# Channel attention on one core: the ones for the sums are loaded into TensorE once instead of before each matmul

## The chip, the cores and the metric

The kernel runs on 1 core of one Trainium2 chip. The metric is the device time in microseconds; a profiled execution also gives the span from the first to the last instruction, which is about 1.8 us shorter. A run counts as slow when it is over 1.5% above the fastest of the same kernel; the results quoted here come from the other, fast ones, except where the text says otherwise. A time or a ratio with two numbers in brackets behind it has its lowest and highest run, or its 95% interval, there. Runs that were submitted together ran on the same chip and share their runs of the kernel before.

## The reference, cut to what matters

```python
def reference(x, w1d):                 # x: 1 x 384 x 384 x 384, bf16;  w1d: 1 value
    g = jnp.einsum("bhwc->bc", x) / (H * W)      # mean of each channel
    s = _sigmoid(g * w1d[0])                     # (written as a convolution of length 1)
    return x * s[:, None, None, :]               # the gate
```

x has 113.25 MB. It has to be read once and written once, 226.5 MB in all, if the kernel does not need x a second time.

## The kernel before

It reads x once. It cuts the 1152 rows per partition into 27 blocks: 25 of 44 rows per partition, then 28 and 24. A block is 128 partitions by up to 16896 bf16 values (4224 KB) and sits in one of six slots of SBUF, the core's working memory. The gate is computed early, from block 0 alone, all blocks are multiplied with that, and the true gate is computed from all sums at the end. Should the two differ in bf16, a second pass over everything repairs the output. On this data they agree, and the second pass does not run.

TensorE makes the sums. A matmul of a 128x128 matrix of ones with 512 columns of a block adds up the partitions. The sums accumulate in PSUM, the memory in which the matmuls put their results: those of block 0 in three of its banks, those of all other blocks in three more. I call the 33 matmuls of a full block a burst.

```python
    def add_rows(place, n, group, first, last):
        n_wide = n * C // WIDE                       # WIDE = 512; 33 for a block of 44 rows
        start = place * C
        for i in range(n_wide):
            bank = acc[group][i % 3]
            plan.op("tensor",
                lambda e, i=i, bank=bank: e.matmul(
                    bank[:, :],
                    ones[:],                          # the weights: always the same ones
                    arena[:, start + i * WIDE : start + (i + 1) * WIDE],
                    start=first and i < 3,
                    stop=last and i >= n_wide - 3,
                ), ...)                               # (cut: what it reads and writes)
```

Each such call becomes two instructions on TensorE, a weight load and a matmul. The main loop, with the waits left to the planner:

```python
    add_rows(places[0], sizes[0], 0, True, True)      # block 0 -> early gate (cut)
    for k in range(1, len(sizes)):
        if k >= n_slots:
            j = k - n_slots
            put(places[j], ...)       # VectorE: gate block j in place; Scalar queue: store it
        if k >= BOTH:
            load(places[k], ...)      # Sync queue: load block k once the slot's store has landed
        add_rows(places[k], sizes[k], 1, k == 1, k == last)
```

So a slot goes through load, sum, gate and store, and the next load waits until the store has landed.

## Time and profile before

| | before |
|---|---|
| median of the first 3 runs | 531.62 us (531.5 to 532.85) |
| span of the profiled execution | 529.9 us |
| bytes moved, mean rate | 226.62 MB, 428 GB/s |
| TensorE matmuls, busy | 865, 246.9 us (47%) |
| TensorE weight loads, busy | 865, 96.4 us (18%) |
| VectorE busy | 241.2 us (46%) |

In the lines of the profile PE is TensorE's matmuls, PEld its weight loads, DVE VectorE, ACT ScalarE and POOL GpSimd; q1, q8 and so on are DMA queues, and SPq and ACTq the queues from which DMAs are issued. L186 is line 186 of the kernel.

From the page of the kernel before: the busy time of each engine; the share of time that the DMA engines were busy in 40 equal slices of the span, in tenths; what they moved; and the DMA queues with packets, bytes and share.

```profile
PE 246.9 (47%) x865; PEld 96.4 (18%) x865; DVE 241.2 (46%) x45; ACT 2.7 (1%) x4; POOL 0.3 (0%) x5
...
DMA  8999999999999999999999999999999999999997
...
DMA packets 8363, 226.62 MB, mean 428 GB/s; under 512 B 930, under 2 KB 930, under 8 KB 930
## 3 DMA queue, kind: packets, MB, share of 16 engines
q10 hardware_dynamic: 4466, 121.90, 53.4%
q1 hardware_dynamic: 3888, 104.60, 46.0%
q8 instruction: 6, 0.10, 0.1%
q14 instruction: 3, 0.02, 0.0%
```

The row of nines is the main reading: the DMA is the limit from the second slice to the last but one.

The costliest groups of the same page (line, engine, operation, shapes, count; then busy time, mean ns of one; then the idle time before them and what ended it):

```profile
L186 PE MATMUL acc<-arena,ones 128*128 128x512 bf16 x864 | 246.8, 457 | 242.3 <-DMA arena<-in_x_dram 242.3
L156 DVE TENSOR_TENSOR arena<-arena,s_early 128x16896 bf16<-128x16896 bf16 (+2 forms) x27 | 234.5, 8691 | 240.3 <-PE acc L186 236.1
L186 PEld LDWEIGHTS acc<-arena,ones 128*128 128x128 bf16 x864 | 96.3, 114 | 392.3 <-DMA arena<-in_x_dram 254.5
```

TensorE waits for loads to land about as long as it works, and VectorE waits for TensorE. Neither is the limit. The Sync queue's own waits show where a slot's time goes: it waits for stores to land before it may load again.

```profile
SPq L99 <- DMA out_dram<-arena: 454.2, 21, 63.1
```

Parts of the chain that ended last, in order of time (start, duration, what): the sums of block 0 near the start, and the sums of the last block with the comparison that follows them.

```profile
14.43 0.16 PE w_all L234
14.59 10.20 PE acc L186 x33
...
497.35 6.27 PE acc L186 x18
...
508.19 0.15 DVE redo L312
```

This chain ends with an instruction at 508 us although the span ends at 529.9: what runs after it are the last stores. In these windows over the end of the span the last two columns are the mean share of the 16 DMA engines that was busy, and GB/s.

```profile
520.00:526.00 6.00, 0.00 (x0) 0.00 (x0) 0.00 (x0) 0.00 (x0) 0.00 (x0) 0.50 0.96 414
526.00:528.00 2.00, 0.00 (x0) 0.00 (x0) 0.00 (x0) 0.00 (x0) 0.00 (x0) 0.50 0.39 166
528.00:536.00 8.00, 0.00 (x0) 0.00 (x0) 0.00 (x0) 0.00 (x0) 0.00 (x0) 0.76 0.01 5
```

### The profile page before, as it was taken

What the parts mean: (1) busy time and instruction counts of PE and PEld (TensorE: products, weight loads), DVE (VectorE), ACT (ScalarE), POOL (GpSimd) and SP (SyncE); (2) the same over time, 40 slices, a digit from 0 to 9 for tenths busy, and PEclk for the clock granted to TensorE, in tenths of its full rate; (3) what the DMA queues carried; (4) which work ended last, traced back from release to release, by engine and by line L of the source; (5) the groups of instructions that cost most, each with busy time, mean ns of one, the idle gap of its engine ahead of it and who ended that gap; (6) DMA issues with size and microseconds to landing.
All of it is one profiled execution on the core that took longest, in us unless ns stands there. A gap on an engine that the chain in (4) does not pass through costs nothing.

```text
span 529.9 us, 1954 instructions
## 1 busy us (share of the span) xinstructions
PE 246.9 (47%) x865; PEld 96.4 (18%) x865; DVE 241.2 (46%) x45; ACT 2.7 (1%) x4; POOL 0.3 (0%) x5
## 2 busy tenths in 40 slices
PE   0977174264274274364264274373263373374400
PEld 0333021121021121121021121121121121121100
DVE  0199824633624624623624615615614615617620
ACT  1000000000000000000000000000000000000000
POOL 0000000000000000000000000000000000000000
PEclk9988675786786875786786875776886876777665
DMA  8999999999999999999999999999999999999997
GB/s 357 430 427 412 446 429 431 446 412 444 434 426 446 413 443 444 416 444 431 429 445 416 441 439 421 446 414 441 444 416 446 427 431 444 424 429 431 444 416 331
DMA packets 8363, 226.62 MB, mean 428 GB/s; under 512 B 930, under 2 KB 930, under 8 KB 930
## 3 DMA queue, kind: packets, MB, share of 16 engines
q10 hardware_dynamic: 4466, 121.90, 53.4%
q1 hardware_dynamic: 3888, 104.60, 46.0%
q8 instruction: 6, 0.10, 0.1%
q14 instruction: 3, 0.02, 0.0%
HBM read 113.25 MB, written 113.25 MB: 427 GB/s over the span
## 4 chain that ended last, share of the span: by engine, by line
another core or an unknown queue 70%; DMA 16%; DVE 4%; PE 3%; issue 1%; SPq 1%; ACT 0%; ACTq 0%
DMA out_dram<-arena 8%; DMA arena<-in_x_dram 6%; PE acc L186 3%; DMA w_one<-in_w1d_dram 2%; DVE arena L156 2%; SPq L91 1%; DVE total L208 1%; ACT s_true L290 0%; ACT s_early L266 0%; DVE total L298 0%; DVE total L206 0%; DVE wrong L306 0%; ACTq L91 0%; SPq L99 0%
## 5 line engine op out<-in xcount | busy, mean ns | idle before, releaser
L186 PE MATMUL acc<-arena,ones 128*128 128x512 bf16 x864 | 246.8, 457 | 242.3 <-DMA arena<-in_x_dram 242.3
L156 DVE TENSOR_TENSOR arena<-arena,s_early 128x16896 bf16<-128x16896 bf16 (+2 forms) x27 | 234.5, 8691 | 240.3 <-PE acc L186 236.1
L186 PEld LDWEIGHTS acc<-arena,ones 128*128 128x128 bf16 x864 | 96.3, 114 | 392.3 <-DMA arena<-in_x_dram 254.5
L234 PE MATMUL w_all<-w_one,ones 1*128 1x1 bf16 x1 | 0.2, 158 | 14.4 <-DMA w_one<-in_w1d_dram 14.4
L243 DVE TENSOR_SCALAR w_scaled<-w_all 128x1 f32<-128x1 f32 x2 | 0.2, 153 | 13.6 <-PE w_all L234 13.6
L208 DVE TENSOR_TENSOR total<-total,acc 128x128 f32<-128x128 f32 (+2 forms) x11 | 4.5, 408 | 1.7 <-PE acc L186 1.4
L206 DVE COPY total<-acc 128x384 f32<-128x384 f32 x1 | 0.6, 556 | 10.0 <-PE acc L186 10.0
L290 ACT ACTIVATE s_true<-total,w_scaled 128x384 bf16<-128x384 f32 x1 | 0.6, 614 | 478.2 <-DVE total L208 478.2
L234 PEld LDWEIGHTS w_all<-w_one,ones 1*128 1x128 bf16 x1 | 0.1, 98 | 14.4 <-issue 14.4
L228 ACT ACT_TABLE_LOAD x1 | 1.3, 1283 | 3.4 <-issue 3.4
L298 DVE TENSOR_TENSOR total<-s_true,s_early 128x384 f32<-128x384 uint16 x1 | 0.6, 557 | 0.7 <-ACT s_true L290 0.7
L266 ACT ACTIVATE s_early<-total,w_scaled 128x384 bf16<-128x384 f32 x1 | 0.6, 614 | 22.7 <-DVE total L208 22.7
L306 DVE TENSOR_REDUCE wrong<-total 128x1 f32<-128x384 f32 x1 | 0.6, 553 | 0.0
L256 DVE MEMSET ones<- 128x128 bf16 x1 | 0.2, 165 | 0.8 <-PEq L386 0.8
L228 ACT ACTIVATE warm<-warm 128x1 f32<-128x1 f32 x1 | 0.2, 203 | 0.0
L312 DVE CAST redo<-wrong 128x1 int32<-128x1 f32 x1 | 0.2, 153 | 0.0
L386 POOL MEMSET const-bfloat16-1.0<- 128x1 bf16 x1 | 0.1, 102 | 0.0
L386 POOL MEMSET const-uint8-127<- 128x1 uint8 x1 | 0.1, 102 | 0.0
L386 POOL MEMSET const-float32-0.0<- 128x1 f32 x1 | 0.1, 99 | 0.2 <-issue 0.2
L386 POOL MEMSET const-float32-1.0<- 128x1 f32 x1 | 0.1, 99 | 0.0
L255 POOL MEMSET warm<- 128x1 f32 x1 | 0.1, 98 | 0.3 <-POOLq L386 0.3
## 6 DMA issues: line engine op xcount, KB each, us to landing
out_dram<-arena ACTq DMA_DIRECT2D x25, 4224.0 KB, 61.5
arena<-in_x_dram SPq DMA_DIRECT2D x21, 4224.0 KB, 39.2
arena<-in_x_dram ACTq DMA_DIRECT2D x4, 2112.0 KB, 27.5
arena<-in_x_dram SPq DMA_DIRECT2D x4, 2112.0 KB, 27.5
arena<-in_x_dram SPq DMA_DIRECT2D x1, 2688.0 KB, 35.6
out_dram<-arena ACTq DMA_DIRECT2D x1, 2688.0 KB, 30.0
arena<-in_x_dram SPq DMA_DIRECT2D x1, 2304.0 KB
out_dram<-arena ACTq DMA_DIRECT2D x1, 2304.0 KB, 27.1
```

The costliest lines, as they stand in the source:

```text
L91: ("op", lambda e: e.dma_start(out, in_), self.pool[i], 16)
L156: return lambda e: e.tensor_tensor(to_v, v, s_b, ALU.mult)
L186: lambda e, i=i, bank=bank: e.matmul(bank[:, :], ones[:], arena[:, start + i * WIDE : start + (i + 1) * WIDE], start=first and i < 3, stop ...
L206: emit = lambda e, part=part, of=of: e.tensor_copy(part, of)
L208: emit = lambda e, part=part, of=of: e.tensor_tensor(part, part, of, ALU.add)
L228: lambda e: e.activation(warm[:, 1:2], warm[:, 0:1], ACT_F.Sigmoid),
L234: lambda e: e.matmul(w_all[:, 0:1], ones[0:1, :], w_one[0:1, 0:1], start=True, stop=True),
L266: lambda e: e.activation(s_early[:], total[:], ACT_F.Sigmoid, scale=w_scaled[:, 0:1]),
L290: lambda e: e.activation(s_true[:], total[:], ACT_F.Sigmoid, scale=w_scaled[:, 1:2]),
L298: lambda e: e.tensor_tensor(total[:], s_true[:].bitcast(U16), s_early[:].bitcast(U16), ALU.not_equal),
L306: lambda e: e.reduce_max(wrong[:], total[:], axis=mybir.AxisListType.X),
L386: nc = _bacc.Bacc("TRN2", target_bir_lowering=False, num_devices=1)
```

## The change

The ones never change, so 863 of the 864 weight loads of the sums repeat what is already in the array. The intent is to load them with the first matmul of the sums, and to emit each later one as a single matmul instruction that says it has no weight load.

```diff
+    loaded = []
+
+    def mm(e, bank, weights, moving, start, stop):
+        if not loaded:
+            loaded.append(e.matmul(bank, weights, moving, start=start, stop=stop))
+            return loaded[0]
+        return e.add_instruction(
+            mybir.InstMatmult(
+                name=nc.get_next_instruction_name(),
+                engine=mybir.EngineType.PE,
+                ins=[e.lower_ap(moving), e.lower_ap(weights)],
+                outs=[e.lower_ap(bank)],
+                start_tensor_calc=start,
+                stop_tensor_calc=stop,
+                ldweights=False,
+            )
+        )
+
     def add_rows(place, n, group, first, last):
...
-                lambda e, i=i, bank=bank: e.matmul(
+                lambda e, i=i, bank=bank: mm(e,
                     bank[:, :],
                     ones[:],
```

One other matmul uses a different load: it spreads the scalar weight over the partitions (w_all), and it comes before the first sum.

## The prediction

> **What bounds the kernel now.** The DMA. The page's slices show the 16 DMA engines at 90% or more in all slices but the first and last, and 433 GB/s nearly throughout 100 to 200 us (the DMA view). 226.62 MB at 433 GB/s are 523 us of the span of 529.9. PE is busy 47%, DVE 46%. The waits agree: PE waits 242 us for loads to land, DVE 236 us for PE, and the sync queue 454 us for stores to land before it reuses a slot.
>
> **What the change removes.** 863 of 864 weight loads of the sums (114 ns each in the list of groups, 96.3 us together). Matmuls, waits, DMAs and DVE work stay, in the same order. But those 96.3 us can't be got back, because the loads overlap the matmuls. Taken from the starts of the matmul records, consecutive matmuls start 215.9 ns apart where the granted clock is 1.0 and mostly 425 to 427 ns apart where it is 0.5. The Trainium skill, "TensorE: Matmul & The Clock Gate", section "Back-to-back issue gap", gives for matmuls alone N/2.4 + 2.5 = 215.8 ns warm and N/1.2 = 426.7 ns cold for N = 512; the trace agrees to a nanosecond although each matmul here has its load. So the stream is paced by its 512 columns and the loads are already free. All I expect is the load in front of a burst: the first matmul starts 0 to 30 ns after it, under 1 us over 26 bursts. A burst of 33 stays at 8.7 to 10.3 us, depending as now on how many matmuls (6 to 14) fall into the half clock.
>
> **How much lies on the critical path.** Almost nothing. In the chain that ended last, the sums are 3% (16.5 us): 10.2 us for block 0 and 6.3 us for the last block. The first does not hold the DMA: six slots of loads, some 60 us of transfer, are queued from the start and the first store is ready at 37 us. The last ends in the check at 508.3 us, while stores run to the span's end. In between a slot goes round in about 120 us (39 load, 10 sum, 9 gate, 61.5 store); a shorter sum would only make a store queue longer.
>
> **Predicted time.** 531.5 us, 8 in 10 between 529.8 and 533.3. Faster by over 2%: 1%. Within 2%: 97%. Slower by over 2%: 2%.
>
> **What would show each step.** Weight loads down from 865 to 2. Matmul starts still 216 ns apart at full clock and 427 at half; PE busy still about 247 us; mean granted clock still about 0.73. PE's wait for loads still about 242 us; 433 GB/s in the middle; the sync queue still waiting about 454 us for stores. The first store still issued at about 37 us, the check done at about 508 us.
>
> **What would make it wrong.** (1) The loads do cost matmul time: bursts shorten by up to 33 x 114 ns = 3.8 us; even so only PE's wait grows and the time stays. (2) The clock grant counts weight loads as work, and bursts run cold: 33 x 427 ns = 14.1 us, still below the 20 us of DMA per block; time the same. (3) The reused weights are not what the sums need, the check finds a difference and the whole second pass runs: the time about doubles. (4) A matmul without its load issues far slower, over 600 ns: a block's sum passes 20 us and PE becomes the limit. I think (3) and (4) improbable.

## The result

| | before | changed |
|---|---|---|
| median of 5 runs | 531.68 us (531.5 to 532.85) | 530.65 us (530.53 to 530.79) |
| ratio, changed to before | | 0.9979 (95%: 0.9967 to 0.9991) |
| span of the profiled execution | 529.9 us | 528.7 us |
| mean granted clock | 0.735 | 0.736 |

Ratios here are the mean time of one kernel's fast runs over that of the other's in the same rounds, so they are not quite the ratio of the medians beside them. By the 2% rule this is "the same", and within the predicted range. But 1.0 us is well outside the spread of the changed kernel's runs, and the interval does not contain 1. It asks for a cause.

From the page of the changed kernel, the lines that answer to those above (the line numbers of the kernel moved; the sums are L184 now):

```profile
PE 245.2 (46%) x865; PEld 0.2 (0%) x2; DVE 241.2 (46%) x45; ACT 2.7 (1%) x4; POOL 0.3 (0%) x5
...
DMA  8999999999999999999999999999999999999998
...
DMA packets 8360, 226.57 MB, mean 429 GB/s; under 512 B 930, under 2 KB 930, under 8 KB 930
## 3 DMA queue, kind: packets, MB, share of 16 engines
q10 hardware_dynamic: 4466, 121.90, 53.5%
q1 hardware_dynamic: 3888, 104.60, 46.1%
q8 instruction: 3, 0.05, 0.0%
q14 instruction: 3, 0.02, 0.0%
...
L184 PE MATMUL acc<-arena,ones 128*128 128x512 bf16 x863 | 244.7, 454 | 244.0 <-DMA arena<-in_x_dram 244.0
L156 DVE TENSOR_TENSOR arena<-arena,s_early 128x16896 bf16<-128x16896 bf16 (+2 forms) x27 | 234.5, 8691 | 240.9 <-PE acc L184 237.5
```

The weight loads are gone (865 to 2), and TensorE is busy as long as before, 245.2 against 246.9 us. It waits for loads as long, 244.0 against 242.3. From the starts of the matmul records, the median from one start to the next is 216.0 ns in both traces. What differs, apart from the loads, is q8: three instruction packets instead of six.

The Sync queue's wait for stores, the pieces of the chain, and the end of the span:

```profile
SPq L99 <- DMA out_dram<-arena: 453.3, 21, 62.7
```

```profile
14.29 0.54 PE acc L182
14.84 8.33 PE acc L184 x32
...
496.39 6.95 PE acc L184 x18
```

```profile
520.00:526.00 6.00, 0.00 (x0) 0.00 (x0) 0.00 (x0) 0.00 (x0) 0.00 (x0) 0.50 0.97 416
526.00:528.00 2.00, 0.00 (x0) 0.00 (x0) 0.00 (x0) 0.00 (x0) 0.00 (x0) 0.50 0.20 83
528.00:536.00 8.00, 0.00 (x0) 0.00 (x0) 0.00 (x0) 0.00 (x0) 0.00 (x0) 0.83 0.00 0
```

Up to 526 us both kernels have moved their data at the same rate. After that, less is left over in the changed kernel (83 against 166 GB/s over the next 2 us) and nothing after 528.

### A closer reading: the sixteen landings of one transfer

The trace shows 16 increments of the semaphore (the counter that tells of a landing) for each transfer of x, and the kernel waits for 16. The Trainium skill, "DMA: Bandwidth & Descriptors", section "Why a DMA increments its semaphore by 16 and not by 1", says why: up to 16 engines finish independently, and each posts its own increment. So the times of the 16 increments show how far the DMA engines of the core are apart, though not which is which. For the last store of each kernel, in us from the span's start, sorted:

```
before   526.3 526.4 526.5 526.5 526.6 526.9 527.2 527.4 527.7 527.7 527.9 527.9 528.0 528.0 529.1 529.4
changed  526.2 526.3 526.3 526.3 526.3 526.4 526.6 526.7 526.7 526.8 526.8 527.2 527.7 528.0 528.1 528.2
```

The first engine is done at the same time in both. The last is 3.04 us behind it before, and 2.00 us in the changed kernel. I call this the lag. The span ends about 0.5 us after the last landing, so the lag accounts for the difference of the spans: 526.3 + 3.04 + 0.5 = 529.8, and 526.2 + 2.00 + 0.5 = 528.7.

The instruction packets of q8 are 16384 bytes each and took 0.88 to 1.07 us. The first of the changed kernel started at 89.4 us. These are landings of the load before it and of the load after it:

```
load landing before it    81.4  83.3 ... 83.5 83.5 83.6  83.7
load landing after it    101.4 103.3 ... 103.6 103.6    104.9
```

One engine has fallen 1.3 us behind the others, and in the later loads it stays 1.1 to 1.3 us behind. After the packets at 229.4 and 389.2 us a second and a third engine are behind.

**Theory F (instruction fetch).** TensorE's program is fetched by the same 16 DMA engines that move x. A fetch of 16 KB occupies one of them for about 1 us. If the work of a transfer is divided equally, that engine stays behind, and a transfer has landed only when its last engine has. Without the weight loads TensorE's program is half as long (56832 bytes compiled instead of 112064), needs three fetches fewer, and the last engine is about 1 us less behind.

**Rival L (the loads themselves).** The loads' reads of SBUF, or their power, slow the DMA a little.

**Rival G (the early gate).** In the changed kernel's trace the first store was issued at 35.6 us instead of 37.2: TensorE started 0.3 us earlier, and in the burst of block 0, 8 instead of 14 distances from one matmul's start to the next were over 380 ns, about half clock. An earlier first store may be what is worth 1 us.

### The profile page after: what moved, and what is told of

The parts are those of the page before. It is cut to its first block, busy times and chain, and to the rows that moved or that the text cites. A ratio compares the mean times of both kernels' runs of the same rounds, so it can differ in the third digit from the quotient of the medians.

```text
span 528.7 us, 1091 instructions
## 1 busy us (share of the span) xinstructions
PE 245.2 (46%) x865; PEld 0.2 (0%) x2; DVE 241.2 (46%) x45; ACT 2.7 (1%) x4; POOL 0.3 (0%) x5
## 4 chain that ended last, share of the span: by engine, by line
another core or an unknown queue 70%; DMA 16%; DVE 4%; PE 3%; SPq 1%; issue 1%; ACT 0%; ACTq 0%
DMA out_dram<-arena 8%; DMA arena<-in_x_dram 6%; PE acc L184 3%; DVE arena L156 3%; DMA w_one<-in_w1d_dram 2%; SPq L91 1%; DVE total L226 1%; ACT s_true L308 0%; ACT s_early L284 0%; DVE total L316 0%; DVE total L224 0%; DVE wrong L324 0%; PE acc L182 0%; ACTq L91 0%
## 5 line engine op out<-in xcount | busy, mean ns | idle before, releaser
L184 PE MATMUL acc<-arena,ones 128*128 128x512 bf16 x863 | 244.7, 454 | 244.0 <-DMA arena<-in_x_dram 244.0
L182 PEld LDWEIGHTS acc<-arena,ones 128*128 128x128 bf16 x1 | 0.1, 105 | 0.0
```

The source lines that it names most:

```text
L182: loaded.append(e.matmul(bank, weights, moving, start=start, stop=stop))
L184: return e.add_instruction(mybir.InstMatmult(name=nc.get_next_instruction_name(), engine=mybir.EngineType.PE, ins=[e.lower_ap(moving), e.l ...
```

## The experiments

All runs were reported correct. In those with wrong sums on purpose that is because the gate rounds to the same bf16 value all the same. It also means that a correct result here does not prove that the sums are right.

### 1. The instructions without the loads (e1_fill1)

One semaphore increment, which nobody waits for, takes the place of each weight load in the program.

```diff
             loaded.append(e.matmul(bank, weights, moving, start=start, stop=stop))
+            loaded.append(nc.alloc_semaphore("filler"))
             return loaded[0]
+        for _ in range(1):
+            e.sem_inc(loaded[1], 1)
         return e.add_instruction(
```

> The changed kernel with one semaphore increment (of a semaphore that nothing waits for) ahead of each matmul that has no weight load: PE's program is as long as before (111872 bytes compiled, before 112064, changed 56832), without the weight loads. Theory F (instruction fetch: each 16 KB fetch for PE takes one of the 16 DMA engines about 1 us, and a transfer has landed only when its last engine has) expects 6 instruction fetches on q8 as before, the slowest engine of the last store about 3.0 us behind the fastest as before (2.0 after), and a ratio to before of 0.9995 to 1.0010. Theory L (the weight loads themselves, their SBUF reads or power, slow the DMA) expects 0.998, as the changed kernel. Theory G (the first store starts earlier) expects 0.998 if the first store is issued near 35.6 us, 1.000 if near 37.2 us.

Measured: 532.42 us (532.17 to 532.53) against 531.75; ratio 1.001 (0.9998 to 1.0023). The gain is gone, though there is no weight load. From the page of this run:

```profile
PE 246.0 (46%) x865; PEld 0.2 (0%) x2; DVE 241.2 (45%) x45; ACT 2.7 (1%) x4; POOL 0.3 (0%) x5
...
q8 instruction: 6, 0.10, 0.1%
```

Six fetches again, and a lag of 3.45 us. The median from matmul to matmul is unchanged, so the increments did not hold TensorE up. L expected 0.998 and falls. The first store was issued at 35.8 us, near the 35.6 of the changed kernel, so G too expected 0.998. F holds. By the medians the run is even 0.7 us slower than before with the same number of fetches, but the interval contains 1, so this is not shown to be a difference. The last engine is 1.9 us behind the one before it; two fetches may have met on one engine, but the trace does not name the engines. That the increments themselves slow the DMA is not excluded by this run alone; runs 6, 10 and 11, with and without increments, speak to it.

### 2. Three increments for each matmul (e2_fill3)

The same with `range(3)`.

> The same with three increments ahead of each matmul: 222336 bytes of PE program. F expects 13 fetches, a still longer lag of the slowest engine (3 to 5 us) and a ratio to before of 1.001 to 1.004. L expects 0.998. If the increments hold up the matmuls (PE burst of 33 over 20 us) the run says nothing; I expect bursts under 14 us.

Measured: 13 fetches, as F expected; but 553.1 to 554.5 us in the fast runs (ratio 1.0417, 1.0399 to 1.0435), and 565 to 570 us in three runs that count as slow. Three increments take 450 ns, so matmuls mostly started 450 ns apart, a burst of 33 took 15 us (I had expected under 14), and at the start TensorE ran almost without a pause until 106 us, behind the loads. One DMA engine ended 15 us behind all others; why is open. Thirteen fetches alone do not explain it: e10_narrow_bare below has as many with a lag of 4.9 us, and here the last engine's distance to the second slowest also grew between fetches (from 15.5 to 18.5 us between the loads that landed at 280 and 304 us, with no fetch between the one at 265.5 and the one at 310.6 us). This run says nothing about F, because TensorE's timing changed with it.

### 3. Half of the matmuls, each with its load (e3_half)

On the kernel before, wrong sums:

```diff
-        for i in range(n_wide):
+        kept = [i for i in range(n_wide) if i % 2 == 0 or i < 3 or i >= n_wide - 3]
+        for i in kept:
             bank = acc[group][i % 3]
```

> The kernel before with about half the matmuls of each block left out (wrong sums on purpose, though the gate rounds to the same value), each of the rest with its weight load: 65472 bytes of PE program, 501 weight loads. F expects 3 fetches and 0.9975 to 0.9985, as the changed kernel. L expects about 0.999, since over half of the loads are still there.

Measured: 530.76 us (530.64 to 530.82), ratio 0.9979 (0.9967 to 0.9992), the same as the changed kernel to the last digit, with 501 weight loads in place. I had expected three fetches and it had four (the fourth at 469 us); the lag was 2.11 us, against 2.00 of the changed kernel.

```profile
PE 170.5 (32%) x501; PEld 61.2 (12%) x501; DVE 241.1 (46%) x45; ACT 2.7 (1%) x4; POOL 0.3 (0%) x5
...
q8 instruction: 4, 0.07, 0.0%
```

With 501 of 865 loads left, L expected about 0.999, which the interval just admits; but together with run 1, which had no loads and no gain, it leaves L nothing. A shorter program gives the gain, with the loads or without.

### 4. Six matmuls a block, no fetch at all (e4_six)

On the changed kernel, `kept = [i for i in range(n_wide) if i < 3 or i >= n_wide - 3]`, wrong sums.

> The changed kernel with only the first three and last three matmuls of each block (wrong sums on purpose): PE's program fits in under 16 KB. F expects no fetch on q8, a lag of the slowest engine of 1 to 2 us at the last store, and 0.996 to 0.998, at or below the changed kernel. L expects 0.998, no further gain, as there were no loads left to take away.

Measured: 529.61 us (529.51 to 529.82), ratio 0.996 (0.9947 to 0.9972): another 1.0 us below the changed kernel, which had no loads to lose. The page has no q8 line any more, the lag is 1.02 us, and the windows over the end show it:

```profile
526.00:528.00 2.00, 0.00 (x0) 0.00 (x0) 0.00 (x0) 0.00 (x0) 0.00 (x0) 0.50 0.02 9
```

TensorE's own work also fell, from 245 to 73.5 us. That this is not the reason is told by run 3: it took 75 us away from TensorE and came out level with the changed kernel.

### 5. A later first store (e5_late)

On the changed kernel, ten matmuls more ahead of block 0's sums, into a bank that is overwritten later:

```diff
+    for _ in range(10):
+        plan.op(
+            "tensor",
+            lambda e: mm(e, acc[1][0][:, :], ones[:], arena[:, 0:WIDE], True, True),
+            reads=["ones"] + rows(places[0], sizes[0]),
+            writes=["acc1"],
+            signal=False,
+        )
     add_rows(places[0], sizes[0], 0, True, True)
```

> The changed kernel with ten more 128x512 matmuls on the first block ahead of its sums, into a bank that is overwritten later: the sums of block 0, the early gate and the first store come 2 to 4.3 us later (first store near 38 to 40 us, before 37.2, changed 35.6). Theory G (the gain came from the earlier first store) expects the gain gone: 1.000 or more. Theory F (number of instruction fetches, 3 as in the changed kernel) and L (no loads) expect 0.998.

Measured: the first store was issued at 38.1 us, later than in either kernel, and the time was 530.63 us (530.34 to 530.78), ratio 0.9978 (0.9965 to 0.9992). Nothing changed: three fetches, a lag of 1.83 us. G falls.

### 6. More fetches, without holding TensorE up (e2b_fill2)

Run 2 with `range(2)`.

> In place of the run with three increments, which held the matmuls up: the changed kernel with two semaphore increments ahead of each matmul, 167104 bytes of PE program. At about 150 ns each, as that run showed, matmuls start some 300 ns apart at full clock and a burst of 33 takes 10 to 12 us, well under the 20 us of DMA per block. F expects 10 fetches, the slowest engine 3.5 to 5 us behind at the last store, and a ratio of 1.001 to 1.004 to before. L expects 0.998.

Measured: ten fetches, 533.52 us (533.46 to 533.61), ratio 1.0033 (1.0019 to 1.0047), a lag of 4.94 us, bursts of 10.15 to 10.41 us. All as F expected.

```profile
q8 instruction: 10, 0.16, 0.1%
```

### 7. Fetches of an engine that has nothing to do (e6_pool)

On the changed kernel, TensorE's program untouched:

```diff
     plan.op("gpsimd", lambda e: e.memset(warm[:, 0:1], 0.0), writes=["warm"])
+    spare = nc.alloc_semaphore("spare")
+    for _ in range(1700):
+        plan.streams["gpsimd"].append(("op", lambda e: e.sem_inc(spare, 1), None, 1))
```

> The changed kernel with 1700 semaphore increments on GpSimd, which has nothing to do: its program grows from 1536 to 110336 bytes, PE's stays. F expects 6 fetches for GpSimd beside 3 for PE, and a loss of 0.5 to 3 us against the changed kernel (ratio to before 0.999 to 1.003), if any engine's fetches cost as PE's do. L and G expect 0.998. If GpSimd's fetches go over DMA engines that are not the last to finish, F expects 0.998 too, and the lag of the slowest engine tells which.

Measured: 537.34 us (537.25 to 537.47), ratio 1.0104 (1.0089 to 1.012). F's direction is right and its size was not: 6.7 us over the changed kernel, where I had expected 0.5 to 3. The page shows what was fetched, and the windows that the end was dragged out:

```profile
q14 instruction: 16, 0.13, 0.1%
q8 instruction: 3, 0.05, 0.0%
```

```profile
528.00:536.00 8.00, 0.00 (x0) 0.00 (x0) 0.00 (x0) 0.00 (x0) 0.00 (x0) 0.50 0.06 26
```

GpSimd was fed by 13 packets of 8192 bytes (I had expected six of 16 KB), one every 8 to 11 us from 9 to 134 us. The landings show one engine that falls back further with each: this is its distance to the second slowest engine, in us, for loads of x that landed in full at these times, and for the last store.

```
landed at    13.8  24.6  35.4  46.1  67.8  89.1  110.4  131.7  152.3  172.2 ...  471.6   last store 535.2
behind       0.74  1.40  2.05  2.70  3.87  4.67   5.33   6.33   6.67   6.62 ...   5.78               4.90
```

It grows as long as the fetches go on, stops when they stop, and over the next 340 us little of it is made up, as the DMA has no pause to make it up in. 106 KB of instructions (13 x 8192 bytes) are 0.05% of the bytes moved, and cost 1.3% of the time, because all went to one engine. Each packet took 0.31 us by its own record, yet the engine lost 0.5 us for each on average (6.67 / 13); why it is more is open.

The increments themselves ran in the same stretch, the last at 137.7 us, so this run alone does not tell the fetches from the increments. The runs on TensorE do: e10_narrow_bare, without any added increment and with 13 fetches, has a lag of 4.86 us, and e2b_fill2, with 1726 increments and ten fetches, 4.94 us. With that, this is the clearest run for the mechanism.

### 8 and 9. Do the loads cost TensorE anything? (e7_four_loads, e8_four_bare)

The prediction said that the loads were hidden behind the matmuls. In these two, each matmul is made four times so that TensorE is the limit, on the kernel before and on the changed one:

```diff
-        for i in range(n_wide):
+        for i, again in [(i, r) for i in range(n_wide) for r in range(4)]:
             bank = acc[group][i % 3]
```

(and `start`, `stop`, `reads` and `signal` apply to the first or last of the four alone).

> The kernel before with each matmul of the sums made four times (sums four times too large on purpose; the gate rounds to the same value), each with its weight load, so that PE is the limit: 132 matmuls per block. If the loads are hidden behind 512 columns as the prediction says, matmuls start 216 ns apart, a block takes 28.5 us and the kernel 760 to 780 us. If a load cost its 114 ns of PE time, matmuls would start some 330 ns apart and the kernel would take about 1150 us.

> The same four times on the changed kernel, without the loads. Hidden loads: 216 ns from start to start and a time within 1% of the run with loads (fetches: 13 against 27, at most some us). Loads that cost: 760 to 780 us, a third less than the run with loads.

Measured, two runs each: 772.35 us with 3457 loads and 771.75 us with 2. The median from start to start is 216.0 ns in both. With TensorE as the limit, the loads are worth nothing measurable either. With 27 fetches against 13 the times are equal too, and the 16 landings of the last store lie within 0.13 us in both: when the DMA has time to spare, an engine that was held up catches up. (The pages count 3388 of the 3457 matmuls, as some records are missing from the traces.)

```profile
PE 745.1 (97%) x3388; PEld 338.8 (44%) x3457; DVE 241.3 (31%) x45; ACT 2.7 (0%) x4; POOL 0.3 (0%) x5
```

```profile
PE 745.4 (97%) x3388; PEld 0.2 (0%) x2; DVE 241.3 (31%) x45; ACT 2.7 (0%) x4; POOL 0.3 (0%) x5
```

### 10 and 11. Narrow matmuls (e9_narrow_loads, e10_narrow_bare)

Each 128x512 matmul as four of 128x128, right sums, one run each (state unknown, as it is one run; clock 0.737 and 0.748 as usual):

```diff
-        for i in range(n_wide):
+        for i, q in [(i, q) for i in range(n_wide) for q in range(4)]:
...
-                    bank[:, :],
+                    bank[:, 128 * q : 128 * q + 128],
                     ones[:],
-                    arena[:, start + i * WIDE : start + (i + 1) * WIDE],
+                    arena[:, start + i * WIDE + 128 * q : start + i * WIDE + 128 * q + 128],
```

> The kernel before with each 128x512 matmul made as four of 128x128, each with its weight load (right sums; 443840 bytes of PE program). A load of 98 to 114 ns no longer hides behind 128 columns: at full clock matmuls start 80 to 115 ns apart, against about 56 ns for the columns alone. F expects 27 fetches and a time of 534 to 540 us, the DMA still being the limit.

> The same narrow matmuls without loads: at full clock about 56 ns from start to start, at half clock 107. F expects 13 fetches and 531 to 535 us, at least 2 us under the narrow run with loads.

Measured: 537.72 us with loads and 533.61 us without, 27 and 13 fetches, lags of 8.92 and 4.86 us. F's times hold. My expectation for TensorE did not: the most frequent distance from start to start is 56 ns in both (55 to 59 ns 2342 times with a load before each matmul, 2428 times without; nearly all the rest is 104 to 107 ns, at half clock). Loads whose records are 114 ns long on average, in this run too, are hidden even behind 128 columns. They also start 56 ns apart, so their records overlap one another: the length of a record is not what a load costs.

### All runs together

Lag is the distance between the first and the last of the 16 landings of the last store, in the profiled execution; the time is the median of all fast runs (one run each for the two narrow kernels, so their state is unknown). Run 2 and the pair in which TensorE is the limit are left out; for run 2 the difference of time and lag would be 537 us, so it does not follow the rule below.

| kernel | fetches on q8 | lag, us | time, us |
|---|---|---|---|
| e4_six | 0 | 1.02 | 529.61 |
| e5_late | 3 | 1.83 | 530.63 |
| changed | 3 | 2.00 | 530.65 |
| e3_half | 4 | 2.11 | 530.76 |
| before | 6 | 3.04 | 531.68 |
| e1_fill1 | 6 | 3.45 | 532.42 |
| e10_narrow_bare | 13 | 4.86 | 533.61 |
| e2b_fill2 | 10 | 4.94 | 533.52 |
| e6_pool | 3, and 13 of 8 KB for GpSimd | 8.89 | 537.34 |
| e9_narrow_loads | 27 | 8.92 | 537.72 |

The time less the lag is 528.4 to 529.0 us in every row. So the time follows the last engine. Between 0 and 27 fetches a fetch for TensorE costs 0.3 us on average, (8.92 - 1.02) / 27, as the kernel waits for the last engine alone.

A measure that does not depend on which engine a fetch falls on is the sum of the 16 distances to the first landing of the last store. It is 6.4 us without a fetch (e4_six), 11.0 with 3 (changed), 18.2 with 6 (before), 23.8 with 10 (e2b_fill2), 27.4 with 13 (e10_narrow_bare) and 51.3 with 27 (e9_narrow_loads): 1.5 to 2.0 us more for each fetch. That is more than the 0.9 to 1.1 us that one packet takes by its record. So a fetch costs the DMA engines more than theory F says; where the rest comes from is open.

## Why the prediction was right, and what it missed

- **"What bounds the kernel now. The DMA."** Right. The DMA row is nines in both pages, and taking 75 us from TensorE's work (run 3) gave no more than the changed kernel has.
- **"The loads are already free."** Right, and now tested where TensorE is the limit: 772.35 against 771.75 us. The comparison with "TensorE: Matmul & The Clock Gate", "Back-to-back issue gap", holds after the change too: 216.0 ns at the median. (That section's other figure, for a stream of loads and matmuls, does not fit; see the list at the end.) That page's section "Step-by-step: what each phase is for" says that the engine pulls weight loads ahead of matmuls in flight, on conditions that no run here tests; this fits, and the runs with 128 columns show that it goes further than I thought.
- **"Matmuls, waits, DMAs and DVE work stay."** This step failed, in one word. The transfers of x stay, but DMA is also what brings TensorE's instructions, and three of six fetches went away. I read the line of q8 as 0.1% of the DMA and left it out of the sum. Its share of the bytes is indeed nothing; what counts is that it falls on one engine of 16 at a time. That term is 1.0 us, all of the measured gain. The range held all the same because the term is smaller than the range is wide (529.8 to 533.3 us), which doesn't make the sum complete.
- **"Almost nothing" on the critical path.** Right for the sums: they were 10.2 us and are 8.9 us at the start of the chain (0.54 + 8.33), and e5_late shows that 2.5 us more there cost nothing. The check was done at 508 us in both.
- **The predicted sizes.** 530.65 us against 531.5, inside 529.8 to 533.3. The sync queue's wait (454.2, now 453.3 us), TensorE's busy time, its wait for loads and the clock are as predicted. "The first store still issued at about 37 us" was wrong, 35.6, and it did not matter. "A burst of 33 stays at 8.7 to 10.3 us" held but for two, at 24.2 and 46.6 us, which ran at full clock throughout and took 7.3.
- **What stays open.** Which DMA engine a fetch falls on; why one engine ended 15 us behind in e2_fill3; where the lag of 1 us without any fetch comes from; and why a fetch costs more than its packet's time. Not every late landing is a fetch's: in the middle of e4_six, which has none, one engine lands its part of each store 2.5 us after the others, and this is gone at the last store. So compare the landings of loads with loads, and of the last store with the last store. And no run here proves that the reused weights are right in every matmul, since the gate rounds to the same value even with half of the sums left out; only the early and the true gate were compared by the kernel, and were equal.

No run gives a correct kernel that is clearly faster than the changed one (e5_late, at 530.63 us, is level with it). The run without fetches, 1.0 us below it, has wrong sums; 864 matmuls of 512 columns, at (112064 - 56832) / 863 = 64 bytes an instruction, are 55296 bytes, which alone is over three blocks of 16 KB. A loop on TensorE, which would make the program shorter, was not tried.

## What to carry to other kernels

In this kernel, whose DMA never pauses, an instruction has a price even on an idle engine: it is fetched by the DMA engines that move the data, and the transfer waits for the engine that was held up. That is about 0.3 us for 256 instructions of TensorE, and 0.5 us for 128 of GpSimd, whose fetches all fall on one engine. In the pair of runs in which the DMA had slack, neither the fetches nor the weight loads cost anything that shows. So in a kernel like this one count instructions, not weight loads, and don't expect much: the change here gave 0.2%.

## What the Trainium skill lacked or had wrong

- "Runtime: NRT & Kernel Launch", "Instruction fetch mechanics", says that a 16 KiB boundary costs one DMA tail-bump, "mostly hidden". Hidden for the engine that executes, yes (216.0 ns from matmul to matmul at the median, with 3, 6 and 27 fetches). In a kernel bound by DMA it is not hidden: 0, 3, 10 and 27 fetches for TensorE gave 529.61, 530.65, 533.52 and 537.72 us.
- The same section gives 16 KiB blocks and names no engine with others. TensorE's packets were 16384 bytes, GpSimd's 8192. That all of GpSimd's fetches slow one and the same DMA engine (6.7 us behind after 13 of them) is on no page that I read.
- "TensorE: Matmul & The Clock Gate", "Back-to-back issue gap", gives about 81 ns for each 128-column and 131 ns for each 512-column matmul in a stream of loads and matmuls. With a load before each matmul the traces show 56 ns and 216 ns at full clock, the figures that it gives for matmuls alone.
- The same page, "LDWEIGHTS (loading the stationary operand)", gives a load as columns/1.2, which is 107 ns for 128. The records are 98 ns at the median (95 to 152), but in e9_narrow_loads the loads start 56 ns apart at full clock, so neither figure is what a load costs in a stream.
- "DMA: Bandwidth & Descriptors", "Why a DMA increments its semaphore by 16 and not by 1", was right and useful: 16 increments for each transfer of x, up to 8.9 us apart at the last store in the runs of the table, 15.7 in e2_fill3.
- On no page that I read: a semaphore increment in TensorE's program takes about 150 ns of its issue (three of them put matmuls 450 ns apart, one was hidden behind 216 ns).
